# Scores from undivided sums of k: the reciprocal denominators move from the normalisation of k into the exponential's factor per partition

## The chip, the cores and the metric

The kernel runs on one core of one Trainium2 chip. The metric is the device time of one execution in microseconds (us); the time of a kernel is the median of its runs. The core has five engines that run beside each other and wait for each other through semaphores: PE (TensorE, matmuls; PEld is its weight load), DVE (VectorE), ACT (ScalarE), POOL (GpSimd) and SP (SyncE, here only DMA issues). Matmul results land in PSUM, which has eight banks of 512 fp32 per partition.

## The reference

Eight batches of eight heads, 576 positions, head size 64, and 32 memory slots. Per batch and head:

```python
a = phi - np.max(phi, axis=2, keepdims=True)
a = np.exp(a)
a = a / (np.sum(a, axis=2, keepdims=True) + 1e-09)
k_m = np.einsum('bhsm,bhsd->bhmd', a, k)
v_m = np.einsum('bhsm,bhsd->bhmd', a, v)
scale = 1.0 / np.sqrt(q.shape[-1])
scores = scale * np.matmul(q, k_m.transpose(0, 1, 3, 2))
scores = scores - np.max(scores, axis=-1, keepdims=True)
attn = np.exp(scores)
attn = attn / (np.sum(attn, axis=-1, keepdims=True) + 1e-09)
return np.matmul(attn, v_m).astype(np.float32)
```

So `a` is a softmax over the positions for each memory slot, `k_m` and `v_m` are the weighted means of k and v for each slot, and the scores of a position are its q against the 32 rows of `k_m`, divided by 8. The result, with the heads side by side, is 4608 rows of 512, and goes through a layer of three weights: `h = max(x@w1, x@w2, x@w3)`, `out = h @ w_out`, with 768 columns in h.

What matters for the change: the mean of k for a slot is a sum of k divided by the slot's denominator, and a score is linear in that mean.

## The kernel before, in words

The kernel writes out the order of its work by hand: a list of steps, each a letter, a number and a batch (`K@2!`), which one function (`issue`, L760) turns into instructions. Every engine gets its instructions in the order of this list, and executes them in that order. A second hand-written list gives each step the PSUM banks that it uses, so a step's first matmul also waits until the earlier user of its banks has been read out. A `!` swaps the engine that reads a result out of PSUM.

For each batch, the steps around the change are these.

- `B` (`att_kv`, L247): 72 small matmuls sum exp(phi)·k, exp(phi)·v and exp(phi)·1 over the positions. The result stays in PSUM with 128 partitions, which are 4 head pairs times 32 slots; the second axis of the result, `a` or `g`, has the two heads of a pair. For batches 0 and 1 the step is cut in two (part 0: denominators and k; part 1: v); for batches 2 to 7 it is one step.
- `N` (`att_kv_norm`, L269): on DVE. A reciprocal of the two denominators per partition into the tile `rden` (L276); v times `rden` into the first third of the tile `kvn` (L280); and, for each of the two heads, k times `rden` into the other two thirds (L291). L291 writes every value twice, since the scores need k in two groups of 32 rows, and sorts even and odd columns of k into two tiles of 128 columns each.
- `K` (`att_kv_t`, L300): three transposes on PE (L306; two in part 0, one in part 1), in which `kvn` is the stationary operand that the weight load reads, and one read-out to `kvt` on ACT or DVE (L177, L181).
- `Q` (`att_q`, L314): transposes of q on DVE (L321).
- `S` (`att_score`, L328): 32 small matmuls (L342) into two pairs of banks, one for each head of a pair, and two exponentials on ACT (L351), 128x576 each, one for each pair of banks. The factor 1/8 is an immediate of the exponential. The partition of a score is again head pair and slot, as in the sums.
- `a`, `s`, `c`, `m`, `X` (or `M`, `R`, `X`) divide the exponentials by their sums over the slots; `D` (`fold`, L472, matmuls L453) multiplies v's means into the weights; `F` (`ffn1`, L496, matmuls L504, read out at L175, L179 and L517), `T` (L681, L690, L699), `t` (`ffn2_begin`, L663), `P` (L615) and the last step (L733, L744) are the layer after the attention.

Between the step `S` of a batch and the next step that uses one of its two pairs of banks stand only a few PE steps: after `S@2` the list has `F1@1 D1@2! ... D0@2 D3@2`, and `D0@2` and `D3@2` write to the two pairs of banks of `S@2`. After `S@3` it is `F9@2` (after `F7@2`, `F5@2`) and `t2@1`; after `S@5` `F1@4` and `F6@4` (after `F11@4`, `F2@4`); after `S@6` `D3@6` and `D1@6`; after `S@7` `F0@6` and `F10@6`.

Loads come through the POOL queue (k, v, q, phi and the weights, which the transfer casts to bf16), results leave through SP and ACT.

Of the kernel before, what the change touches and what calls it, by code (L numbers as in the profile page):

```python
# [11 lines left out]
ALU = mybir.AluOpType  # L12
# [3 lines left out]
def kernel(  # L16
# [12 lines left out]
    nc = tc.nc  # L29

    B, H, S, D = q.shape
    M = phi.shape[-1]
    P = 128
    NP = H // 2
    NG = NP // 2
    HP = P // 2
    NC = S // HP
    R = 32
# [46 lines left out]
    def load_ph(b):  # L85
        ph = inp.tile([P, NP, NC, M], FP32, name="ph", tag="ph")
        loaded.setdefault(b, {})["ph"] = ph
        dst = ph.rearrange("p j c m -> p j (c m)")
        if b == 0:
            for h in halves:  # L90
                nc.sync.dma_start(out=dst[:, h], in_=by_pair(phi, b)[:, h])
        else:
            nc.gpsimd.dma_start(out=dst, in_=by_pair(phi, b))

    def load_kv(b, i, h=slice(0, NP)):
        kv = vs[b % 3] if i else ks[b % 2]
        nc.gpsimd.dma_start(  # L97
            out=kv[:, h].rearrange("p j c d -> p j (c d)"),
            in_=by_pair((k, v)[i], b)[:, h],
        )  # L100

    def pack(b, swap):
        out_, in_ = krs[b % 3][:, :, :, 0:D], ks[b % 2]
        if swap:
            nc.scalar.copy(out=out_, in_=in_)
        else:
            nc.gpsimd.tensor_copy(out=out_, in_=in_)  # L107

    def load_q(b, h=slice(0, NP)):
        if "q" not in loaded.setdefault(b, {}):  # L110
            loaded[b]["q"] = inp.tile([P, NP, NC, D], BF16, name="qq", tag="qq")
        nc.gpsimd.dma_start(  # L112
            out=loaded[b]["q"][:, h].rearrange("p j c d -> p j (c d)"),
            in_=by_pair(q, b)[:, h],
        )

    def load_w(i):
        w = (moe_w1, moe_w2, moe_w3)[i]
        nc.gpsimd.dma_start(  # L119
            out=w_sb[:, :, i], in_=w.rearrange("(j p) f -> p j f", p=P)  # L120
        )

    ident = const.tile([P, P], BF16, name="ident")

    def load_wo():
        nc.gpsimd.dma_start(out=wo_sb, in_=moe_w_out.rearrange("(t p) c -> p t c", p=P))
# [26 lines left out]
    def one_bank():  # L153
        return psum[:, int(next(banks))]

    def two_banks():
        i = int(next(banks))
        return psum[:, i : i + 2]
# [12 lines left out]
    def evacuate(kind, n, swap, out_, in_, relu=False):  # L171

        if (EVAC[kind][n] == "a") != swap:
            if relu:
                nc.scalar.activation(out=out_, in_=in_, func=AF.Relu)  # L175
            else:
                nc.scalar.copy(out=out_, in_=in_)  # L177
        elif relu:
            nc.vector.tensor_scalar_max(out=out_, in0=in_, scalar1=0.0)  # L179
        else:  # L180
            nc.vector.tensor_copy(out=out_, in_=in_)  # L181
# [84 lines left out]
                        tile_position=(HP * a, M * j),  # L266
                    )

    def att_kv_norm(b, part=None):  # L269

        s = st[b]
        kvp = s["kvp", part]
        if part != 1:
            rden = s["rden"] = work.tile([P, NG], FP32, name="rden")
            s["kvn"] = work.tile([P, 3, P], BF16, name="kvn")
            nc.vector.reciprocal(out=rden, in_=kvp[:, :, 0 if part == 0 else D])  # L276
        rden, kvn = s["rden"], s["kvn"]
        if part != 0:
            v0 = 0 if part == 1 else D + 1
            nc.vector.tensor_tensor(  # L280
                out=kvn[:, 0].rearrange("p (a d) -> p a d", a=NG),
                in0=kvp[:, :, v0 : v0 + D],
                in1=rden.unsqueeze(2).to_broadcast([P, NG, D]),
                op=ALU.mult,
            )
        if part == 1:
            return
        k0 = D if part == 0 else 0
        for g in range(NG):
            kn = kvn[:, 1:3, HP * g : HP * (g + 1)]  # L290
            nc.vector.tensor_scalar_mul(  # L291
                out=kn.rearrange("p h (t d) -> p h t d", t=2),
                in0=kvp[:, g, k0 : k0 + D]
                .rearrange("p (d h) -> p h d", h=2)
                .unsqueeze(2)
                .to_broadcast([P, 2, 2, R]),
                scalar1=rden[:, g : g + 1],
            )

    def att_kv_t(b, swap, part=None):  # L300

        s = st[b]
        ns = {None: slice(0, 3), 0: slice(1, 3), 1: slice(0, 1)}[part]
        ps = one_bank().bitcast(BF16)[:, 0 : 3 * P].rearrange("p (n m) -> p n m", n=3)
        for n in range(3)[ns]:
            nc.tensor.transpose(ps[:, n], s["kvn"][:, n], ident)  # L306
        if part != 1:
            s["kvt"] = work.tile([P, 3, P], BF16, name="kvt")
        evacuate("K", 0, swap, s["kvt"][:, ns], ps[:, ns])
        if b == 0 and part != 0:  # L310
            s["kvtn"] = const.tile([P, P], BF16, name="kvtn")
            nc.scalar.mul(out=s["kvtn"], in_=ps[:, 0], mul=-1.0)
# [15 lines left out]
    def att_score(b):  # L328

        s = st[b]  # L330
        kvt, qT = s["kvt"], s["qT"]
        e2 = s["e2"] = work.tile([P, NG, S], BF16, name="e2")
        if b // 2 not in attns:
            x = hts[b // 2] = work.tile([P, FT + NG, 2 * S], BF16, name="hx")
            attns[b // 2] = x.rearrange("p (i k) n -> p i k n", i=NG)[:, :, FT // NG]
        sc = [two_banks() for _ in range(NG)]
        for h in range(2):
            for j in range(NP):
                for a in range(NG):
                    for t in range(2):  # L340
                        r = slice(R * (2 * a + t), R * (2 * a + t + 1))
                        nc.tensor.matmul(  # L342
                            sc[a][M * j : M * (j + 1), t, 0:SH],
                            lhsT=kvt[r, 1 + h, M * j : M * (j + 1)],
                            rhs=qT[r, j, :, :, h],
                            start=(h == 0),
                            stop=(h == 1),
                            tile_position=(R * (2 * a + t), M * j),
                        )
        for a in range(NG):  # L350
            nc.scalar.activation(  # L351
                out=e2[:, a].rearrange("p (t r c) -> p t r c", t=2, c=NC),
                in_=sc[a][:, :, 0:SH].rearrange("p t (c r) -> p t r c", c=NC),
                func=AF.Exp,
                scale=0.125,
            )

    def ones_sum(b, g):
# [401 lines left out]
    def issue(b, n, swap):  # L760

        i = int(n[1:]) if len(n) > 1 else None
        {
            "I": lambda: [make_identity(nc, ident)]
            + [nc.gpsimd.memset(x[:, :, :, D:], 1.0) for x in krs],
            "Y": lambda: load_w(i) if i < 3 else load_wo(),
            "L": lambda: load_ph(b) if i == 0 else load_q(b) if i == 3 else load_kv(b, i - 1),
            "J": lambda: load_q(b, halves[i]),
            "H": lambda: load_kv(b, i % 2, halves[i // 2]),
            "h": lambda: load_kv(b, 0, slice(i, i + 1)),  # L770
            "r": lambda: pack(b, swap),
            "E": lambda: [att_exp(b, h) for h in (halves if b == 0 else [slice(0, NP)])],
            "B": lambda: att_kv(b, i),
            "N": lambda: att_kv_norm(b, i),
            "K": lambda: att_kv_t(b, swap, i),
            "Q": lambda: att_q(b, i),
            "S": lambda: att_score(b),
            "a": lambda: att_t(b, i),
            "s": lambda: att_sum(b, i),
            "c": lambda: att_rec(b, i),  # L780
            "m": lambda: att_mul(b, i, swap),
            "X": lambda: (ones_mul if (b, i) in ONES else att_back)(b, i),
            "M": lambda: ones_sum(b, i),
            "R": lambda: ones_rec(b, i),
            "D": lambda: fold(b, i, swap),
            "F": lambda: ffn1(b, i, swap),
            "T": lambda: ffn2(b, i, swap),
            "U": lambda: combine_w(b, i, swap),
            "A": lambda: combine_a(b, i, not swap),
            "P": lambda: products(b, i, swap),  # L790
            "W": lambda: w3_t(i, swap),
            "g": lambda: send(i),
            "d": lambda: fold_begin(i),
            "t": lambda: ffn2_begin(b, i),
            "O": lambda: w3_o(i, swap),
            "V": lambda: w_diff(i, swap),
            "Z": lambda: warm_up(i),
        }[n[0]]()


    for w in """
# [28 lines left out]
        n, b = w.rstrip("!").split("@")  # L830
# [31 lines left out]
```

## Time and profile before

| | us |
|---|---|
| median of 3 runs (160.28 to 160.69) | 160.58 |
| the profiled execution | 160.41 |
| its span, first to last instruction | 158.6 |
| PE busy in the span | 150.2 (95%) |
| DVE busy | 118.4 (75%) |
| ACT busy | 98.4 (62%) |
| POOL busy | 105.1 (66%) |

The mean granted clock of TensorE is 1.000. The profile comes from one execution; 1.8 us of its 160.41 lie outside the span. In the lines of a profile, `out<-in xcount` names what an instruction writes and reads by the program's tiles; `psum` is the one PSUM tile, `128x576` is partitions by elements, and `L351` is a line of the kernel. A line of the timeline is: start in us, length in us, engine, line, operation, tiles, shapes, count of merged instructions, and in brackets the idle time of the engine before it with what ended that. The chain of work that ended last is followed back from the last instruction.

### The profile page before, as it was taken

What the parts mean: (1) busy time and instruction counts of PE and PEld (TensorE: products, weight loads), DVE (VectorE), ACT (ScalarE), POOL (GpSimd) and SP (SyncE); (2) the same over time, 40 slices, a digit from 0 to 9 for tenths busy, and PEclk for the clock granted to TensorE, in tenths of its full rate; (3) what the DMA queues carried; (4) which work ended last, traced back from release to release, by engine and by line L of the source; (5) the groups of instructions that cost most, each with busy time, mean ns of one, the idle gap of its engine ahead of it and who ended that gap; (6) DMA issues with size and microseconds to landing.
All of it is one profiled execution on the core that took longest, in us unless ns stands there. A gap on an engine that the chain in (4) does not pass through costs nothing.

```text
span 158.6 us, 5184 instructions
## 1 busy us (share of the span) xinstructions
PE 150.2 (95%) x2228; PEld 100.0 (63%) x2228; DVE 118.4 (75%) x205; ACT 98.4 (62%) x140; POOL 105.1 (66%) x100
## 2 busy tenths in 40 slices
PE   6996798999899999999999999999999999999992
PEld 2342544673456548646777577787874888888871
DVE  2032802789998997897998889899999868899851
ACT  4206335753787799997787789888976934124210
POOL 7960101993039959949969998999979996910000
PEclk9999999999999999999999999999999999999999
DMA  5999999999999999999999999999803500331544
GB/s 153 162 199 208 206 209 213 281 207 209 205 283 218 301 236 235 315 263 283 276 223 208 230 371 231 250 184 186 262 0 136 198 6 0 132 132 70 198 160 171
DMA packets 22934, 31.78 MB, mean 200 GB/s; under 512 B 1152, under 2 KB 18560, under 8 KB 22912
## 3 DMA queue, kind: packets, MB, share of 16 engines
q0 software_dynamic: 16128, 21.43, 71.3%
q1 hardware_dynamic: 6064, 8.85, 15.6%
q10 hardware_dynamic: 720, 1.18, 2.2%
q8 instruction: 17, 0.28, 0.7%
q14 instruction: 5, 0.04, 0.1%
HBM read 39.32 MB, written 9.44 MB: 307 GB/s over the span
## 4 chain that ended last, share of the span: by engine, by line
PE 66%; DMA 23%; POOL 7%; issue 2%; ACT 1%; POOLq 0%
PE psum L504 24%; PE psum L615 24%; DMA w_sb<-in_moe_w_dram 14%; DMA kvr<-in_v_dram 10%; PE psum L453 4%; PE psum L681 4%; PE psum L256 3%; PE psum L663 2%; POOL ko L97 2%; PE psum L342 2%; POOL qq L112 1%; POOL kvr L97 1%; PE psum L690 1%; PE psum L699 1%; POOL w_sb L119 1%
## 5 line engine op out<-in xcount | busy, mean ns | idle before, releaser
L504 PE MATMUL psum<-hx,wp 128*128 128x288 bf16 x384 | 53.2, 286 | 0.1
L504 PEld LDWEIGHTS <-wp 128*128 128x128 bf16 x384 | 36.4, 98 | 11.7 <-issue 2.1
L517 DVE TENSOR_TENSOR hx<-psum,h 128x576 bf16<-128x576 f32 x48 | 34.9, 750 | 6.1 <-PE psum L504 5.0
L177 ACT CAST wp<-psum 128x1024 bf16<-128x1024 f32 (+1 forms) x29 | 27.5, 993 | 3.6 <-PE psum L453 3.4
L175 ACT ACTIVATE h<-psum 128x576 bf16<-128x576 f32 x34 | 21.5, 656 | 7.5 <-PE psum L504 6.8
L615 PEld LDWEIGHTS <-hx 128*128 128x128 bf16 x192 | 18.4, 98 | 3.5 <-issue 1.1
L164 PE MATMUL psum<-warm 128*128 128x512 bf16 x44 | 12.5, 440 | 1.2 <-DVE warm L131 1.2
L351 ACT ACTIVATE e<-psum 128x576 bf16<-128x576 f32 x16 | 9.5, 649 | 5.9 <-PE psum L342 5.9
L107 POOL COPY kvr<-ko 128x2304 bf16<-128x2304 bf16 x3 | 6.3, 2113 | 10.2 <-DMA ko<-in_k_dram 10.2
L615 PEld LDWEIGHTS <-w_sb 128*128 128x128 bf16 x120 | 11.6, 98 | 2.3 <-issue 0.7
L321 DVE STREAM_TRANSPOSE qT<-qq 128x576 f32<-128x576 f32 x16 | 11.8, 758 | 0.7 <-DMA qq<-in_q_dram 0.7
L629 ACT COPY snap<-psum 128x512 f32<-128x512 f32 x11 | 6.5, 595 | 8.7 <-PE psum L615 8.7
L540 POOL TENSOR_TENSOR w_sb<-hx 128x1024 bf16<-128x1024 bf16 x5 | 10.6, 2123 | 1.5 <-DVE hx L517 1.5
L218 POOL TENSOR_TENSOR w_sb<-w_sb 128x2048 bf16<-128x2048 bf16 x1 | 4.1, 4062 | 10.4 <-PE psum L453 10.4
L179 DVE TENSOR_SCALAR h<-psum 128x576 bf16<-128x576 f32 x14 | 10.3, 746 | 0.7 <-PE psum L504 0.6
L234 ACT ACTIVATE e<-ph 128x1152 bf16<-128x1152 f32 (+1 forms) x9 | 9.6, 1068 | 1.7 <-DMA ph<-in_phi_dram 1.6
L615 PE MATMUL psum<-wo_sb,hx 128*128 128x256 bf16 x72 | 9.8, 273 | 0.0
L615 PE MATMUL psum<-w3T,hx 128*128 128x256 bf16 x72 | 9.8, 273 | 0.0
L540 POOL TENSOR_TENSOR twb<-wp 128x256 bf16<-128x256 bf16 x11 | 7.4, 676 | 3.5 <-ACT wp L177 3.5
L177 ACT COPY ot<-psum 128x512 f32<-128x512 f32 x9 | 5.3, 595 | 7.0 <-PE psum L690 6.1
L647 DVE TENSOR_TENSOR ot<-psum,snap 128x512 f32<-128x512 f32 x12 | 8.2, 684 | 1.8 <-PE psum L615 1.1
L427 POOL TENSOR_TENSOR t<-t,sm 128x1152 bf16<-128x1152 bf16 x4 | 8.5, 2137 | 1.5 <-DVE sm L420 1.0
(104 smaller groups left out, 283.8 us busy)
## 6 DMA issues: line engine op xcount, KB each, us to landing
out_dram<-ot SPq DMA_DIRECT2D x8, 512.0 KB, 5.4
qq<-in_q_dram POOLq DMA_DIRECT2D x7, 576.0 KB, 10.4
ph<-in_phi_dram POOLq DMA_DIRECT2D x7, 576.0 KB, 13.8
ko<-in_k_dram POOLq DMA_DIRECT2D x7, 576.0 KB, 16.9
kvr<-in_v_dram POOLq DMA_DIRECT2D x7, 576.0 KB, 11.3
out_dram<-ot SPq DMA_DIRECT2D x14, 256.0 KB, 2.2
w_sb<-in_moe_w_dram POOLq DMA_DIRECT2D x3, 768.0 KB, 18.2
out_dram<-ot ACTq DMA_DIRECT2D x4, 256.0 KB, 6.7
```

The costliest lines, as they stand in the source:

```text
L164: nc.tensor.matmul(po[:, 0:BANK], lhsT=warm[:, 0:P], rhs=warm, start=True, stop=True)
L175: nc.scalar.activation(out=out_, in_=in_, func=AF.Relu)
L177: nc.scalar.copy(out=out_, in_=in_)
L179: nc.vector.tensor_scalar_max(out=out_, in0=in_, scalar1=0.0)
L234: nc.scalar.activation(out=s["e"][:, js], in_=loaded[b]["ph"][:, js], func=AF.Exp)
L321: nc.vector.transpose(out=s["qT"][:, j].rearrange("p j c r e -> p (j c r e)").bitcast(FP32), in_=loaded[b]["q"][:, j].rearrange("p j c d - ...
L351: nc.scalar.activation(out=e2[:, a].rearrange("p (t r c) -> p t r c", t=2, c=NC), in_=sc[a][:, :, 0:SH].rearrange("p t (c r) -> p t r c", ...
L427: (nc.vector if swap else nc.gpsimd).tensor_tensor(out=t, in0=t, in1=x.to_broadcast(list(t.shape)), op=ALU.mult,)
L504: nc.tensor.matmul(acc[:, h, 0:SH], lhsT=wps[b][:, g, w * DF + ft * P : w * DF + (ft + 1) * P], rhs=attn[:, g, c0 : c0 + SH], start=(g == ...
L517: nc.vector.tensor_tensor(out=hT[:, row(ft), (b % 2) * S : (b % 2 + 1) * S].rearrange("p (h n) -> p h n", h=2), in0=a, in1=s["h1", ft], op ...
L540: eng.tensor_tensor(out=out_, in0=in0, in1=in1, op=op)
L615: nc.tensor.matmul(po[:, q * CH : (q + 1) * CH], lhsT=lhs(k, q), rhs=rhs(k), start=(i < 3 and k == 0 and q == 0), stop=(k == KT and q == 1 ...
```

## The change

The sums of k are no longer divided. For batches 2 to 7, and in part 0 of batches 0 and 1, one instruction multiplies the sums of both heads by 0.125 and writes them to `kvn`, each head's 64 columns twice in a row. The reciprocal comes behind this copy and not ahead of it, and v's multiplication behind the reciprocal. The even and odd columns of k are no longer sorted by this instruction; the transposes read `kvn` with a step of two elements instead. The exponential of the scores takes `rden`, one value per partition for its head, as its factor, where it had the immediate 0.125. The step `N` is never swapped in the list of steps, so the copy is DVE's in every batch. The list of steps and the list of banks stay as they are.

```diff
-    def att_kv_norm(b, part=None):
+    def att_kv_norm(b, swap, part=None):
...
         if part != 1:
             rden = s["rden"] = work.tile([P, NG], FP32, name="rden")
             s["kvn"] = work.tile([P, 3, P], BF16, name="kvn")
+            k0 = D if part == 0 else 0
+            kn = s["kvn"][:, 1:3].rearrange("p x (y d) -> p x y d", x=NG, y=2)
+            k_ = kvp[:, :, k0 : k0 + D].unsqueeze(2).to_broadcast([P, NG, 2, D])
+            if swap:
+                nc.scalar.mul(kn, k_, 0.125)
+            else:
+                nc.vector.tensor_scalar_mul(kn, k_, 0.125)
             nc.vector.reciprocal(out=rden, in_=kvp[:, :, 0 if part == 0 else D])
-        rden, kvn = s["rden"], s["kvn"]
-        if part != 0:
-            v0 = 0 if part == 1 else D + 1
-            nc.vector.tensor_tensor(
-                out=kvn[:, 0].rearrange("p (a d) -> p a d", a=NG),
-                in0=kvp[:, :, v0 : v0 + D],
-                in1=rden.unsqueeze(2).to_broadcast([P, NG, D]),
-                op=ALU.mult,
-            )
-        if part == 1:
+        if part == 0:
             return
-        k0 = D if part == 0 else 0
-        for g in range(NG):
-            kn = kvn[:, 1:3, HP * g : HP * (g + 1)]
-            nc.vector.tensor_scalar_mul(
-                out=kn.rearrange("p h (t d) -> p h t d", t=2),
-                in0=kvp[:, g, k0 : k0 + D]
-                .rearrange("p (d h) -> p h d", h=2)
-                .unsqueeze(2)
-                .to_broadcast([P, 2, 2, R]),
-                scalar1=rden[:, g : g + 1],
-            )
+        v0 = 0 if part == 1 else D + 1
+        nc.vector.tensor_tensor(
+            out=s["kvn"][:, 0].rearrange("p (a d) -> p a d", a=NG),
+            in0=kvp[:, :, v0 : v0 + D],
+            in1=s["rden"].unsqueeze(2).to_broadcast([P, NG, D]),
+            op=ALU.mult,
+        )
 
     def att_kv_t(b, swap, part=None):
...
+        kn = s["kvn"][:, 1:3].rearrange("p x (d h) -> p h (x d)", h=2)
         for n in range(3)[ns]:
-            nc.tensor.transpose(ps[:, n], s["kvn"][:, n], ident)
+            nc.tensor.transpose(ps[:, n], kn[:, n - 1] if n else s["kvn"][:, 0], ident)
...
                 func=AF.Exp,
-                scale=0.125,
+                scale=s["rden"][:, a : a + 1],
             )
...
-            "N": lambda: att_kv_norm(b, i),
+            "N": lambda: att_kv_norm(b, swap, i),
```

## The prediction

> **What bounds the kernel now.** I read the page first: busy times, the slices, the chain.
>
> ```profile
> PE 150.2 (95%) x2228; PEld 100.0 (63%) x2228; DVE 118.4 (75%) x205; ACT 98.4 (62%) x140; POOL 105.1 (66%) x100
> PE   6996798999899999999999999999999999999992
> PE 66%; DMA 23%; POOL 7%; issue 2%; ACT 1%; POOLq 0%
> ```
>
> PE is 9 in all slices but the first few, and the chain runs through PE and DMA; DVE is not in it, ACT holds 1%. Next I read the chain in order of time, to see where DMA hands over to PE.
>
> ```profile
> 34.91 15.17 DMA kvr<-in_v_dram
> 50.08 0.14 issue
> 50.22 0.80 PE psum L256 x72
> ```
>
> Up to 50.1 us the chain is a transfer: v of batch 2, for which PE waits at 50.22. Behind it the chain is PE nearly without a break to 155.6. The waits of PE from 50 us on have one entry:
>
> ```profile
> PE psum L256 <- DMA kvr<-in_v_dram: 0.3, 1, 0.3
> ```
>
> That list leaves out short stalls. I found those in the timeline of PE, by starts against a steady pace (four L504 take 0.49 us in the chain, so 0.122 each; eight L615 take 0.87, so 0.109). So the tail of 105 us is bound by PE's own work, and a change of DVE or ACT counts only where PE stops for it.
>
> **The change part by part.**
>
> *DVE's step N.* The timeline of DVE in batch 2:
>
> ```profile
> 51.14 0.17 DVE L276 RECIPROCAL rden<-psum 128x2 f32<-128x2 f32 x1 [0.56 <-PE psum L256]
> 51.34 0.29 DVE L280 TENSOR_TENSOR kvn<-psum,rden 128x128 bf16<-128x128 f32 x1
> 51.55 0.60 DVE L291 TENSOR_SCALAR kvn<-psum,rden 128x128 bf16<-128x128 f32 x2
> ```
>
> The four instructions take from 51.14 to 52.15, 1.01 us. Afterwards there are three: a copy of 256 elements, the reciprocal, v's product. DVE's copies from PSUM to bf16 or fp32 (L181) take 0.68 us for 128x512 and 1.19 for 128x1024, so 0.255 for 256 elements and 0.17 fixed: the copy takes 0.43, and its successor starts about 0.08 before its end, as L280's does (0.29 long, next start 0.21 later): 0.35. Then 0.20 for the reciprocal and 0.29 for the product: 0.84 us, so 0.17 less for each of six batches. Off the path: K's transposes follow two L504 groups that end at 51.17 + 8 x 0.122 = 52.15 in PE's own order, the moment at which DVE ends now. In the other batches N ends 0.9 us or more ahead of K. In batch 0's part 0 the copy alone releases K, 0.4 us sooner, but S waits there for q (DVE's L321 sat 0.72 idle for its DMA). In batch 1, K waits 0.06 for DVE, ahead of the transfer that PE awaits anyway. What runs behind N on DVE starts 0.17 sooner; only at D1 of batch 2 (54.20, behind the L517 that ends at 54.14) does PE stand for that chain, 0.08, and the next fold waits for an exponential anyway. I count 0 gained, with 0.1 as the bound.
>
> *The transposes* read `kvn` with a step of two elements as weights, twice a batch.
>
> ```profile
> L306 PEld LDWEIGHTS <-kvn x24: 95/98/98, 10.6 to 114.1; 128*128 128x128 bf16 x24
> L342 PE MATMUL psum<-qT,kvt x256: 282/295/309, 12.8 to 122.1; 32*32 32x288 bf16 x128
> ```
>
> No weight load of before has a step. Three transposes take 0.17 us in the chain, 57 ns each, so a load fits in 57 now. If a step of two halved its rate, each would take up to 114: 12 x 57 ns = 0.68 us in batches 2 to 7. The nearest row is L342, whose moving operand qT is read with just that step: 295 ns for 288 columns against 286 for L504's without one. I take 0, with 0.68 as the upper end; a gain is excluded, since as many columns are loaded.
>
> *The exponentials* get a factor per partition instead of an immediate. No ACT row of before has such an operand.
>
> ```profile
> L351 ACT ACTIVATE e<-psum x16: 644/651/657, 13.4 to 123.0; 128x576 bf16<-128x576 f32 x16
> ```
>
> Call d what the operand adds to each. It can't be below 0, as the same 576 elements pass. On DVE the nearest row with such an operand is L291: 0.343 us for 128 elements from PSUM, against 0.292 for L280 without one: 0.05 more (its pattern has more dimensions, which may be part of it). On ACT itself the nearest row is what the start of an instruction costs: two exponentials in a row take 1.19 where 2 x 0.65 = 1.30 would be the sum, so 0.11 of the second lies under the first. If the operand is one more access at the start, that is its size. I take the middle of these two, d = 0.08, and 0 and 0.11 as ends. The second of a pair then ends 2d later.
>
> The Trainium skill, ScalarE: Activation LUTs, section What ACT_TABLE_LOAD costs, speaks against the change here: each such operand adds about 93 ns to an ACTIVATE, where an immediate adds nothing. By that d the sum below would be 0.63; before's rows show only the immediate side.
>
> Where does PE wait for an exponential? S takes two pairs of banks, which later steps may fill only when the exponential has read them. The timelines of ACT (first line) and PE after S of batch 2, and then of batch 6:
>
> ```profile
> 53.64 1.19 ACT L351 ACTIVATE e<-psum 128x576 bf16<-128x576 f32 x2 [0.63 <-PE psum L342]
> ```
>
> ```profile
> 54.20 0.63 PE L453 MATMUL psum<-w_sb,kvt 64*32 64x512 bf16 x16
> 54.88 0.41 PE L453 MATMUL psum<-w3o,kvt 64*32 64x512 bf16 x8
> ```
>
> ```profile
> 110.71 1.19 ACT L351 ACTIVATE e<-psum 128x576 bf16<-128x576 f32 x2 [0.31 <-PE psum L342]
> ```
>
> ```profile
> 111.72 0.44 PE L453 MATMUL psum<-w3o,kvt 64*32 64x512 bf16 x8
> 111.95 0.42 PE L453 MATMUL psum<-w_sb,kvt 64*32 64x512 bf16 x8
> ```
>
> Batch 2: the pair ends at 54.83, and D3 starts at 54.88, 0.05 later; that 0.05 I take as the step from ACT to PE. Batch 6: ends 111.90, D1 starts 111.95. Both are released by the second exponential with no slack, and pay 2d each. The other batches, as PE's start less the exponential's end less 0.05: batch 3, t2 at 66.54, second ends 66.35, slack 0.14 (the first has 0.19); batch 5, F6 at 93.44, second ends 93.33, slack 0.06 (first 0.11); batch 7, F0 at 123.21, first ends 123.14, slack 0.02; batch 4, F1 at 80.93, first ends 80.37, slack 0.5. With d = 0.08, in the order of batches 2, 6, 3, 5, 7: 0.16 + 0.16 + 0.02 + 0.10 + 0.06 = 0.50 us, all in the tail that PE bounds. With d = 0.05 it is 0.27, with 0.11 0.77.
>
> In batch 1 the ones-sum (L363, 40.98) also follows the second exponential (ends 40.93), 2d = 0.16; PE then comes later to the wait for v at 50.22. That gap is 0.55 from the last L504's start at 49.67, of which a change to a small tile needs 0.22: 0.33 free, which covers it. In batch 0 transfers of weights (PE idle for w_sb at 15.87) cover it.
>
> *The waits.* The first exponential now waits for DVE's reciprocal too; that ended some 2 us before (51.6 against 53.64), since scores need K, and K needs v's product behind it. Read-outs of h and wp queued behind it on ACT (62% busy) shift by 2d and find idle time soon. The order on every engine is otherwise the same; no DMA moves past another on SP, ACT or POOL.
>
> **Sum.** 0 (DVE) + 0 (loads) + 0.50 = 0.50 us. On the profiled execution, span 158.6 and 160.41 in all, that gives 160.91. The median of the runs is 0.17 above that execution, so on the median 160.58 + 0.50 = 161.1.
>
> **The rivals.**
>
> 1. *The operand costs nothing that PE sees*: its fetch lies under the instruction ahead, or in the 0.3 to 1.2 us for which ACT idles ahead of most pairs. For it: that idle time, and the overlap of 0.11. Against: no slack in batches 2 and 6, and DVE's 0.05. Then 160.6, and at best, with the 0.08 at batch 2 given back, 160.5: not slower. It decides by d: with 2d under 0.05 the sum is under 0.1, and up to d = 0.078 it stays under 0.48. If only the first of a pair pays d, the sum is 0.08 + 0.08 + 0.02 + 0.06 = 0.24, 160.8.
> 2. *The stepped weight loads run at half rate.* For it: half of what is fetched is not used. Against: qT's row. Up to 0.68 more: 161.3 with rival 1, 161.8 with the forecast.
> 3. *N does not get shorter*, because the copy of 256 elements written twice runs slower than DVE's other read-outs from PSUM. L291 takes 2.7 ns an element with its fixed part; by that the copy is 0.69, N as long as before or up to 0.1 longer, and K of batch 2, which has no slack, up to 0.1 later: 161.2.
>
> **How the numbers follow.** Forecast (d from 0.05 to 0.11, loads unchanged, rival 3 within it): 0.50, time 161.1, own range 160.8 to 161.4. Rival 1 with the half payment: 0.26. Rival 2: 0.17. What the profile does not show: 0.07, mostly a head that lands its transfers otherwise, either way. The range is 160.4 to 161.8. A difference of 0.3% (0.48 us) is about what a measurement here can tell from none; the forecast lies just above it. Slower by more: six tenths of the forecast, nearly all of rival 2, some of the rest: 0.50. Within: 0.43. Faster: 0.07, since PE's stalls in the tail that this change could touch sum to 0.1.
>
> **What would show it.** The exponentials' row (L346 afterwards) rises from 651 to about 730 ns and the pairs from 1.19 to about 1.35; the gap ahead of D3 in batch 2 and of D1 in batch 6 grows by 0.16. The transposes still take 57 ns each. N takes 0.84 us from the copy's start to the product's end. The transfer still lands at 50.1. Wrong are: a row of 651 (rival 1), transposes of 100 ns or more (rival 2), or a landing that moves by more than 0.3 us.

## The result: 161.40 us against 160.62, and the profile after

| | before | after |
|---|---|---|
| median of 12 runs, us | 160.62 (160.28 to 161.14) | 161.40 (160.86 to 162.05) |
| ratio to before | | 1.0045, 95% interval 1.0028 to 1.0061 |
| profiled execution, us | 160.41 | 161.61 |
| its span, us | 158.6 | 159.8 |
| first sum of batch 2 starts, us | 50.22 | 50.85 |
| from there to the start of the last 12 matmuls, us | 103.94 | 104.48 |

The changed kernel is slower, by 0.78 us of medians (the interval of the ratio is 0.45 to 0.98 us). The two profiled spans differ by 1.15. The last two rows of the table split that: 0.63 lie in the head, which ends with a transfer, and 0.54 in the tail, where PE sets the pace. In what follows "the tail" is the last row. The granted clock is no cause: its mean is 1.000 before and 0.999 after, and 1.000 in a second profile of the changed kernel with a tail 0.57 us longer than before's. Of the runs of `e1_pointer_only` and `e2_copy_only` below, one each (163.77 and 162.95 us) was slow, over 1.5% above the fastest of its kernel, and it is left out of their medians and ratios. The ends of the tail, in the chain of before and then of after:

```profile
154.16 1.43 PE psum L744 x12
```

```profile
50.85 0.80 PE psum L256 x72
...
155.33 1.43 PE psum L739 x12
```

From the profile page of the changed kernel, the busy times, the chain's shares, and the group of the exponentials, and then the exponentials' row by source (minimum, median and maximum in ns):

```profile
PE 150.0 (94%) x2219; PEld 100.1 (63%) x2228; DVE 117.0 (73%) x197; ACT 99.3 (62%) x140; POOL 105.0 (66%) x100
...
PE 65%; DMA 23%; POOL 7%; issue 2%; ACT 1%; POOLq 0%
...
L346 ACT ACTIVATE e<-psum,rden 128x576 bf16<-128x576 f32 x16 | 11.0, 737 | 6.3 <-PE psum L337 6.3
```

```profile
L346 ACT ACTIVATE e<-psum,rden x16: 732/740/746, 13.4 to 124.2; 128x576 bf16<-128x576 f32 x16
```

DVE works 1.4 us less (8 instructions fewer), ACT 0.9 more, PE as much as before. Apart from the longer exponentials (740 ns, 651 before) nothing here shows a loss, and the chain's shares have hardly moved. The busy times of DVE and ACT together fell, and the kernel became slower. The place of the loss is seen in the chain in order of time, here of after and then of before:

```profile
34.78 15.93 DMA kvr<-in_v_dram
...
54.29 0.35 ACT e L346
54.65 0.27 issue
54.91 0.74 ACT e L346
```

```profile
54.20 0.65 ACT e L351
```

v of batch 2 lands at 50.72, later than the 50.08 of before (that is the head). And both exponentials of batch 2 are now pieces of the chain. In the chain of before only the second was, from 54.20 to 54.84, behind PE's own work. The timelines of ACT and then of PE behind the scores of batch 2, and the same for batch 6, in the changed kernel:

```profile
54.27 1.37 ACT L346 ACTIVATE e<-psum,rden 128x576 bf16<-128x576 f32 x2 [0.63 <-PE psum L337]
...
111.65 1.37 ACT L346 ACTIVATE e<-psum,rden 128x576 bf16<-128x576 f32 x2 [0.32 <-PE psum L337]
```

```profile
54.71 0.77 PE L448 MATMUL psum<-w_sb,kvt 64*32 64x512 bf16 x16
55.70 0.41 PE L448 MATMUL psum<-w3o,kvt 64*32 64x512 bf16 x8 [0.22 <-ACT e L346]
...
112.66 0.44 PE L448 MATMUL psum<-w3o,kvt 64*32 64x512 bf16 x8
113.07 0.41 PE L448 MATMUL psum<-w_sb,kvt 64*32 64x512 bf16 x8
```

The pair takes 1.37 us (1.19 before). In batch 2 it ends at 55.64, and D3 starts at 55.70. In batch 6 it ends at 113.02, and D1 starts at 113.07, 0.41 behind the step ahead of it (0.23 before). As before, PE goes on 0.05 us behind the second exponential, and that exponential ends 0.18 later.

### Where the 0.54 us arise

The time from the first score of one batch to the first score of the next (by the starts of L342 and L337 on PE) cuts the tail into six stretches; what lies between the start of the tail and the first score of batch 2 is the same to 0.02. Each holds the steps that take over the banks of the first batch's scores. The middle rows are what the prediction's slacks give for an operand of d on both exponentials of a pair, the others are differences to the kernel before, in us (`e3` is told below; in it each exponential has two such operands). The sums are of unrounded times and can differ by 0.01 from those of the rows.

| stretch | 2 to 3 | 3 to 4 | 4 to 5 | 5 to 6 | 6 to 7 | 7 to end | sum |
|---|---|---|---|---|---|---|---|
| after, measured | 0.18 | 0.03 | -0.01 | 0.11 | 0.16 | 0.07 | 0.54 |
| slacks, d = 0.08 (the prediction) | 0.16 | 0.02 | 0 | 0.10 | 0.16 | 0.06 | 0.50 |
| slacks, d = 0.18 | 0.36 | 0.22 | 0 | 0.30 | 0.36 | 0.16 | 1.40 |
| `e3`, measured | 0.38 | 0.22 | -0.01 | 0.29 | 0.35 | 0.16 | 1.39 |

### The profile page after: what moved, and what is told of

Its sections match the earlier page's. It is cut to its first block, busy times and chain, and to the rows that moved or that the text cites. A ratio compares the mean times of both kernels' runs of the same rounds, so it can differ in the third digit from the quotient of the medians.

```text
span 159.8 us, 5170 instructions
## 1 busy us (share of the span) xinstructions
PE 150.0 (94%) x2219; PEld 100.1 (63%) x2228; DVE 117.0 (73%) x197; ACT 99.3 (62%) x140; POOL 105.0 (66%) x100
## 4 chain that ended last, share of the span: by engine, by line
PE 65%; DMA 23%; POOL 7%; issue 2%; ACT 1%; POOLq 0%
PE psum L610 23%; PE psum L499 23%; DMA w_sb<-in_moe_w_dram 13%; DMA kvr<-in_v_dram 10%; PE psum L448 4%; PE psum L676 4%; PE psum L256 3%; PE psum L658 2%; POOL ko L97 2%; PE psum L337 2%; POOL qq L112 1%; POOL kvr L97 1%; PE psum L685 1%; PE psum L694 1%; POOL w_sb L119 1%
## 5 line engine op out<-in xcount | busy, mean ns | idle before, releaser
L346 ACT ACTIVATE e<-psum,rden 128x576 bf16<-128x576 f32 x16 | 11.0, 737 | 6.3 <-PE psum L337 6.3
L282 DVE TENSOR_SCALAR kvn<-psum 128x256 bf16<-128x256 f32 x8 | 3.4, 419 | 11.1 <-PE psum L256 11.0
```

Source lines behind the costliest of these rows:

```text
L346: nc.scalar.activation(out=e2[:, a].rearrange("p (t r c) -> p t r c", t=2, c=NC), in_=sc[a][:, :, 0:SH].rearrange("p t (c r) -> p t r c", ...
```

## The experiments

**The theory**: the operand per partition makes each exponential longer, and PE waits for that in the stretches where the slack behind the scores is short; the shorter N and the stepped transposes give and take nothing. **The rivals**: the other parts of the change carry the loss (transposes, copy, or a later head), or the first exponential's new wait for the reciprocal does.

The tail of every kernel, by the same two rows of the chain as in the table above, beside the medians. The kernel before was timed anew beside each group of runs: its median was 160.62 beside after, 160.74 beside `e1_pointer_only` to `e4`, 160.92 beside `e1_again` and `e6` to `e8`, and 160.77 beside `e5` and `e9`. A time of the table is compared with that one; the ratio comes from the single runs, and so differs a little from that of the two medians.

| kernel | median, runs | ratio, 95% interval | tail | less before |
|---|---|---|---|---|
| before | | | 103.94 | |
| after | 161.40, 12 | 1.0045, 1.0028 to 1.0061 | 104.48 | 0.54 |
| `e1_pointer_only` | 161.36, 5 | 1.0039, 1.0024 to 1.0054 | 104.71 | 0.77 |
| `e1_again` | 161.36, 1 | | 104.69 | 0.75 |
| `e2_copy_only` | 160.57, 11 | 0.9996, 0.9983 to 1.0008 | 103.96 | 0.02 |
| `e3_two_pointers` | 162.10, 6 | 1.0090, 1.0074 to 1.0106 | 105.32 | 1.38 |
| `e4_after_moved` | 161.38, 6 | 1.0049, 1.0031 to 1.0068 | 104.60 | 0.66 |
| `e6_one_product` | 160.58, 12 | 0.9981, 0.9964 to 0.9999 | 103.96 | 0.02 |
| `e7_second_only` | 161.06, 1 | | 104.12 | 0.18 |
| `e8_first_only` | 161.25, 1 | | 104.19 | 0.25 |
| `e5_after_rounds` | 161.23, 12 | 1.0026, 1.0011 to 1.0042 | 104.51 | 0.57 |
| `e9_one_product_rounds` | 160.93, 12 | 1.0006, 0.9986 to 1.0025 | 103.93 | -0.01 |

### The operand alone, and the rest alone

`e1_pointer_only` is the kernel before; its exponential reads the same 0.125 from a tile.

```diff
+    eighth = const.tile([P, 1], FP32, name="eighth")
+    nc.vector.memset(eighth, 0.125)
...
-                scale=0.125,
+                scale=eighth,
```

> The kernel before, with one edit: the exponential's factor 0.125 is read from a tile of one value per partition and not given as an immediate. Theory A (the operand costs about 0.09 us an exponential, and PE waits for it where it has no slack): the exponentials take about 740 ns against 651, PE's tail from the first sum of batch 2 to the end of the span grows by 0.5 us, and the ratio to before is 1.003 to 1.004, as much as the whole change costs. Rival B (the undivided sums and the transposes with a step cost the time): the tail is as before within 0.1 us, and the ratio 1.000.

`e2_copy_only` is the changed kernel without the operand.

```diff
-                scale=s["rden"][:, a : a + 1],
+                scale=1.0,
```

> The changed kernel, with the exponential's factor the immediate 1.0 in place of the reciprocal denominators, so that the scores' division is left out; the undivided copy, the order on DVE and the stepped transposes stay. Theory A: exponentials at 651 ns, tail as before within 0.1 us, ratio 1.000, since N's 0.17 us saved on DVE releases nothing. Rival B: the tail grows by 0.5 us, ratio 1.003 to 1.004, and the exponentials are at 651 all the same. If the undivided copy gains on DVE what the operand hides, the ratio is below 0.998.

The two halves fall on the two sides of the table: the operand alone costs as much as the change (ratio 1.0039), the other parts nothing (0.9996). The rows of the exponential's line, by source, in `e1_pointer_only` and in `e2_copy_only` (minimum, median and maximum in ns):

```profile
L353 ACT ACTIVATE e<-psum,eighth x16: 732/740/745, 13.4 to 124.1; 128x576 bf16<-128x576 f32 x16
```

```profile
L346 ACT ACTIVATE e<-psum x16: 645/650/659, 13.4 to 123.4; 128x576 bf16<-128x576 f32 x16
```

740 against 650 ns, with a value that is written once at the start: the length comes from the operand, not from a wait for the reciprocal. That rival falls.

In five of the six stretches `e1_pointer_only` loses what the changed kernel loses, to 0.01 us. It has 0.23 us more in its tail than the changed kernel, nearly all of it ahead of the scores of batch 6 (that stretch is 0.32 longer than before, in the changed kernel 0.11). So the ratio of 1.0039 holds some 0.2 us that the change does not have. `e1_again` is the same kernel once more.

> The kernel before with the factor 0.125 read per partition, once more, for its trace: the first trace had 0.21 us ahead of batch 6's scores that the changed kernel's does not have. If that belongs to the kernel, it is there again; if it was that execution's, the tail is 0.5 us over before's, as in the changed kernel.

It came again, so it belongs to that kernel. The scores of batch 6 wait there for DVE to read out F9 of batch 5. The timelines of DVE in `e1_pointer_only` and in the changed kernel:

```profile
110.09 1.54 DVE L519 TENSOR_TENSOR hx<-psum,h 128x576 bf16<-128x576 f32 x2 [0.36 <-ACT h L177]
```

```profile
110.10 0.76 DVE L512 TENSOR_TENSOR hx<-psum,h 128x576 bf16<-128x576 f32 x1
```

The first read-out starts there behind 0.36 us of idle time, but the ACT instruction that the trace names had ended 0.2 earlier. What it waited for stays open.

### Two operands

`e3_two_pointers` gives the exponentials of the changed kernel a second operand, a bias of zeros.

```diff
+                bias=zero,
                 scale=s["rden"][:, a : a + 1],
```

> The changed kernel, with a second operand per partition on the same exponentials: a bias of zeros read from a tile, not an immediate. Theory A with the slacks of before (0, 0, 0.14, 0.06 and 0.02 us in batches 2, 6, 3, 5 and 7): d rises from 0.09 to 0.18, exponentials to about 830 ns, the tail to 1.4 us over before's (0.36 + 0.36 + 0.22 + 0.30 + 0.16), 0.9 over the change's; time near 162.2. A plain proportion (each 0.09 worth 0.5 us) would give 1.0 over before. Rival B: as the changed kernel, 0 over it.

```profile
L348 ACT ACTIVATE e<-psum,zero,rden x16: 821/830/837, 13.6 to 124.6; 128x576 bf16<-128x576 f32 x16
```

The lengths go 651, 740, 830: 89 and 90 ns, so each operand pays by itself, on these instructions of 128x576. The Trainium skill, ScalarE: Activation LUTs, section What ACT_TABLE_LOAD costs, gives some 93 ns for an operand of one value per partition; these rows agree to 4 ns. The stretches (table above) follow the slacks of before to 0.02 us in each: batch 3 had 0.14 of slack, which hid nearly all of the first operand and nothing of the second. In the list of PE's waits from 50 us on, the changed kernel and then `e3_two_pointers` (us in total, times, longest):

```profile
PE psum L448 <- ACT e L346: 0.2, 1, 0.2
```

```profile
PE psum L451 <- ACT e L348: 0.5, 2, 0.3
```

The list shows only the long stalls: of 0.54 us lost it has 0.2, of 1.38 it has 0.5. The rest is in gaps that one sees only by comparing starts.

### One exponential of the pair

`e7_second_only` keeps the operand on the second of a pair, `e8_first_only` on the first; the other has an immediate 1.0, so that head's sums stay undivided.

```diff
-                scale=s["rden"][:, a : a + 1],
+                scale=s["rden"][:, a : a + 1] if a else 1.0,   (e7_second_only)
+                scale=1.0 if a else s["rden"][:, a : a + 1],   (e8_first_only)
```

> The changed kernel, where only the second exponential of a pair has the operand; the first has the immediate 1.0, so one head of each pair goes undivided. Theory A with d = 0.09 and the slacks of before: batch 2 0.09, batch 6 0.09, batch 5 0.03, batch 3 0 and batch 7, where PE waits for the first exponential, 0: the tail is 0.21 us over before's. A cost of the operand that lies under the first exponential would give 0 here.

> The changed kernel, where only the first exponential of a pair has the operand; the second has the immediate 1.0, so the other head of each pair goes undivided. Theory A: the second exponential starts 0.09 later and is no longer, so batch 2 0.09, batch 6 0.09, batch 5 0.03, batch 3 0, and batch 7 now pays 0.07: the tail is 0.28 us over before's.

The line's rows in `e8_first_only`, first those with the operand:

```profile
L346 ACT ACTIVATE e<-psum,rden x8: 740/740/747, 13.7 to 123.3; 128x576 bf16<-128x576 f32 x8
L346 ACT ACTIVATE e<-psum x8: 642/642/652, 14.4 to 123.9; 128x576 bf16<-128x576 f32 x8
```

Tails of +0.18 and +0.25, by the slacks 0.21 and 0.28. Batches 2 and 6 lose 0.07 to 0.09 in each of the two, so there the delays of the pair add up. Batch 7 loses 0.07 with the first alone and nothing with the second: there PE takes over the first exponential's banks, as the prediction had it. The slacks give 0.03 too much in both sums; it lies in batches 6 and 5, a hundredth or two each.

### Moving the waiting steps

`e4_after_moved` is the changed kernel with another step put between the scores and each of the two steps that wait with no slack, in the list of steps and in that of banks.

```diff
-D0@2 D3@2 t3@1 T3@1
+D0@2 t3@1 D3@2 T3@1
...
-D3@6 D1@6! P0@4 P1@4
+D3@6 P0@4 D1@6! P1@4
```

> The changed kernel, with two steps moved in the hand-written order, banks with them: batch 2's D3 stands behind t3 of batch 1 and not ahead of it, and batch 6's D1 behind P0 of batch 4, so that PE has 0.9 and 1.0 us of other matmuls before it needs the banks that the second exponential reads. Theory A (PE waits for the exponential): the waits at these two places go, 0.42 us (0.18 of the change's and 0.24 that the kernel before had too) and 0.18 us; the tail falls 0.6 us under the change's, to before's, and the time to 160.8. Rival B (PE's own work got longer): the tail falls by 0.24 at most.

This failed: the tail is 0.12 longer than the changed kernel's, not shorter. PE's timeline in batch 2:

```profile
54.13 0.77 PE L448 MATMUL psum<-w_sb,kvt 64*32 64x512 bf16 x16
55.05 1.02 PE L658 MATMUL psum<-wo_sb,hx 128*128 128x512 bf16 x4
56.01 0.41 PE L448 MATMUL psum<-w3o,kvt 64*32 64x512 bf16 x8
```

L658, moved ahead, starts 0.53 us behind the last L448 ahead of it; in the changed kernel, where nothing makes it wait, 0.32. Its bank had held F1 of batch 1, which DVE read out until 55.00; L658 starts 0.05 later. The wait for ACT became a wait for DVE, 0.21 us long. And each place now has two changes more between the fold's matmuls (L448, on tiles of 64x32) and matmuls over the whole array. By the starts on PE without the waits, that makes the sequence in batch 2 0.22 us longer (0.32 + 0.31 + 0.32 in place of 0.19 + 0.32 + 0.22) and in batch 6 0.26 (0.34 + 0.20 + 0.32 in place of 0.17 + 0.32 + 0.11). The waits for the exponentials did go, as theory A had it: 0.42 less in batch 2 and 0.18 less in batch 6. With what came in their place that leaves 0.01 and 0.08 more than the changed kernel has, and the stretches from these batches to the next are 0.02 and 0.08 longer. A slack can't be had by exchanging two steps here; the expectation had counted PE's work and left out the bank of the moved step and the changes of shape.

### The division in one product, with the immediate kept

`e6_one_product` computes the same result in another way: the two products of before become one, which reads the reciprocals of both heads by broadcast; the stepped transposes of the change stay, and the exponential keeps 0.125. The diff is against the changed kernel; its copy and the reciprocal behind it go.

```diff
+            nc.vector.reciprocal(out=rden, in_=kvp[:, :, 0 if part == 0 else D])
...
+            rd = rden.unsqueeze(2).unsqueeze(3).to_broadcast([P, NG, 2, D])
+            nc.vector.tensor_tensor(out=kn, in0=k_, in1=rd, op=ALU.mult)
...
-                scale=s["rden"][:, a : a + 1],
+                scale=0.125,
```

> The reference's result by another way: the sums of k of both heads are divided by one product with the reciprocal denominators (a tensor_tensor, broadcast over the 64 columns and the two copies), the transposes keep their step, and the exponential has its immediate 0.125 again. So DVE has three instructions in N as in the changed kernel, and no operand per partition is on ACT. Theory A: exponentials at 651 ns, PE's tail from the first sum of batch 2 as before within 0.1 us, ratio to before 1.000, and 0.5 us under the changed kernel. Rival B (the undivided sums or the step cost the time): 0.5 us over before.

DVE's timeline in batch 2:

```profile
51.78 0.17 DVE L276 RECIPROCAL rden<-psum 128x2 f32<-128x2 f32 x1 [1.46 <-PE psum L256]
51.98 0.42 DVE L281 TENSOR_TENSOR kvn<-psum,rden 128x256 bf16<-128x256 f32 x1
52.32 0.28 DVE L285 TENSOR_TENSOR kvn<-psum,rden 128x128 bf16<-128x128 f32 x1
```

The product with the division in it takes 0.42 us, no more than the copy without it. So the division was free on DVE once both heads shared an instruction, and only moving it to ACT had a price. The tail is that of before. The interval of its ratio, 0.9964 to 0.9999, just leaves 1 out, so this kernel was measured a second time, and the changed kernel beside it. The two texts that follow count the tail to the end of the span, some 4.5 us more than the tables here.

> The kernel in which one product divides k for both heads by the reciprocals and the exponential keeps its immediate, once more, for whether it beats the kernel before. Theory: its tail is that of the kernel before (108.43 against 108.42), so its median lies within 0.1 us of it, ratio 0.9994 to 1.0006, and the 0.9981 of its first look was scatter of the head. Rival: its shorter work on DVE (by 0.1 to 0.2 us a batch) lets the head land sooner; then the ratio is about 0.998 again, 0.3 us less.

> The changed kernel itself once more, for the size of its loss. Theory: the loss is the 0.54 us that PE waits in the tail behind the first sum of batch 2, and what the medians showed above it (0.78) is the scatter of the moment at which v of batch 2 lands, which differs from execution to execution whatever the kernel. Then the difference of medians lies at 0.5 to 0.6, ratio about 1.0034, and the tail is 108.94 again. Rival: the change also delays the head, by some 0.2 us; then the difference is 0.75 to 0.8 again, ratio 1.005.

The second measurement gives 1.0006 (0.9986 to 1.0025) for the one product: the same as before. In the tail it is better than the changed kernel by all that this one lost (0.58 us), in the medians by 0.30. None of these kernels is shown to beat the kernel before: the 0.9981 did not come again. The changed kernel comes out at +0.46 us of medians (interval of the ratio 0.18 to 0.68 us) and a tail of +0.57. The two differences of medians, 0.78 and 0.46, lie on both sides of the tail's 0.54. A head later by 0.2 us would give 0.75 to 0.8, which the second interval leaves out and the first does not. Each half of the change speaks against it too: `e2_copy_only`, with the new N and transposes, lies between 0.27 us under and 0.13 over before by its ratio, and `e1_pointer_only`, with the operand, is 0.63 over by its ratio where its tail alone is 0.77. A later head is not seen; one of 0.1 us could not be told from the scatter. Where the head ends, by the chains of `e5_after_rounds` (the same kernel as the changed one) and of `e9_one_product_rounds`:

```profile
34.95 15.45 DMA kvr<-in_v_dram
...
50.53 0.80 PE psum L256 x72
```

```profile
32.66 8.31 DMA kvr<-in_v_dram
...
51.51 0.80 PE psum L256 x72
```

The changed kernel's first sum of batch 2 started at 50.85 and at 50.53 in its two profiles, the other kernel's (`e6` and `e9`) at 50.85 and at 51.51; in the last the chain leaves the DMA a batch earlier, at v of batch 1. The 0.63 us in the head of the two first profiles is of the size of this scatter.

## Why the prediction was right, step by step

- **The exponentials' operand**: right in mechanism, nearly in size. d is 0.089 us, taken as 0.08; the sum 0.54, taken as 0.50. The bounds 0.05 and 0.11 held, but the 0.08 is the middle of two rows that do not measure this operand (one of DVE, and the overlap of two exponentials), so that it came within 0.01 is in part luck. With d = 0.089 the slacks give 0.58; batches 3, 5 and 6 lost a hundredth or two less than that. The overlap stayed: the second of a pair started 0.104 before the first's end in before (651 - 547) and 0.101 in after (740 - 639), so nothing of the operand is hidden under the instruction ahead. The Trainium skill, ScalarE: Activation LUTs, section What ACT_TABLE_LOAD costs, has 93 ns for such an operand, the closer d. By it the prediction's slacks give 0.62 (0.186 + 0.186 + 0.046 + 0.126 + 0.073) and not the 0.63 that the prediction states; that overshoots.
- **The slacks**: right for each batch, and at twice the operand too (`e3`). This was the step that carried the forecast. Two sums under rival 1 are a little low (by the slacks 0.105 for d = 0.025 and 0.482 for d = 0.078), which changes nothing. Rival 1 (PE sees nothing) falls by the 740 ns, its half payment by `e7`, in which the second exponential alone pays, and by the 732 ns or more of all sixteen.
- **N**: right. From 51.78 to 52.60 in the changed kernel's DVE timeline, 0.82 us against the 0.84 expected and 1.01 before; the copy takes 0.42, taken as 0.43. Rival 3 falls. The gain in time is 0 (`e2`, `e6`, `e9`: tails of 0.02, 0.02, -0.01). One reading was wrong, without effect: in batch 7 N ends 0.41 us ahead of K (113.65 and 114.06 in before), not 0.9 or more.

```profile
51.78 0.42 DVE L282 TENSOR_SCALAR kvn<-psum 128x256 bf16<-128x256 f32 x1 [1.45 <-PE psum L256]
52.12 0.16 DVE L283 RECIPROCAL rden<-psum 128x2 f32<-128x2 f32 x1
52.31 0.29 DVE L287 TENSOR_TENSOR kvn<-psum,rden 128x128 bf16<-128x128 f32 x1
```

- **The transposes with a step of two**: right, nothing. The weight loads of the changed kernel take as long as before, and three transposes take 0.17 or 0.18 us in the chains of both kernels, batch by batch the same. Rival 2 falls.

```profile
L301 PEld LDWEIGHTS <-kvn x24: 95/98/99, 10.3 to 115.2; 128*128 128x128 bf16 x24
```

- **The head**: the step that was wrong. The prediction took the landing of v of batch 2 as fixed at 50.1 and a shift by over 0.3 us as a sign against itself. It landed at 50.72, with the forecast mechanism in place all the same. In the profiles of all kernels the sum behind it starts anywhere from 50.22 to 51.51, so one profile's landing can be no sign either way. The three profiles with the N of before lie at 50.22 to 50.45, the nine others at 50.28 to 51.51; the ratio of `e2` above shows no delay from that. The prediction added its sum to a median, which averages over most of this, and so the error cost it little: 161.1 against 161.40 and, in the second measurement, 161.23. But 161.40 is the very edge of its own range of 160.8 to 161.4, with 0.24 us of the 0.78 outside its mechanism; that the scatter was no larger is luck.

## What to carry to other kernels

A factor per partition that is folded into an ACTIVATE is not free: here it lengthened each exponential of 128x576 by 0.09 us, whether it was a constant or the reciprocals. Other sizes were not tried. What it costs is read from the slack between the end of the instruction and the step that waits for its buffers, batch by batch. Before a division is moved off an engine, look whether that engine can do it within an instruction it needs anyway; here one product with a broadcast took as long as the copy. And compare spans only from a point behind the last load that scatters: here 0.54 us of cause stood beside 0.63 of scatter in a single pair of profiles.

## What the runs showed of the hardware that was not expected

- On DVE, 128x256 from PSUM to bf16 took 0.42 us both as a copy with an immediate and as a product with a broadcast operand, while the product of before with its factor per partition took 0.34 for 128 elements, and the broadcast product of v 0.29 for as many.
- From a matmul over the whole array to a fold matmul on tiles of 64x32, PE took 0.20, 0.22 and 0.31 us from start to start, behind matmuls of 256, 288 and 512 columns that follow each other at 0.109, 0.122 and 0.216: 0.09 us more in each case. From a fold matmul to the whole array it took 0.31 to 0.34, where the next fold starts 0.17 to 0.20 behind (`before`, `e4_after_moved`).
